# Two of three state corrections from TensorE matmuls to ScalarE products and VectorE sums, with a new instruction order

## Chip, cores, metric

The kernel runs on one core of a Trainium2 chip. The metric is the device time of one execution in microseconds (us). Shorter names, as the profile uses them: PE is TensorE (PEld its weight loads), DVE is VectorE, ACT is ScalarE, POOL is GpSimd, SP is SyncE, which issues nearly all DMAs.

## What is computed

Two independent layers over S = 2048 tokens of width D = 448, side by side in one output of width 896. All inputs and the output are bf16.

```
# A: sliding-window attention, 16 heads of 28; each token sees itself and 7 others, 2 tokens apart
qkv = x @ wqkv
logits = q . k[t - 2w] * 28**-0.5,  w = 0..7   (masked where t - 2w < 0)
a = (softmax(logits) . v[t - 2w]) @ wo
# B: a diagonal complex state-space layer with 448 states
dt = exp(log_dt); Lam_bar = exp(dt * Lam); B_bar = ((Lam_bar - 1) / Lam) * B
h[t] = Lam_bar * h[t-1] + B_bar @ x[t]
b = 2 * Re(C @ h[t]) + x * Dskip
out = concat(a, b)
```

## The kernel before, in words

Every piece of work is a small function marked `@op`, and the program is the list `ORDER`: a loop at the end of the kernel calls the functions in that order. In `QK021@32` the digits are arguments and what follows `@` are the PSUM banks; a trailing `.` lets ScalarE do an eviction, `=` lets VectorE do it. Each engine runs its own instructions strictly in the sequence in which `ORDER` emits them, and waits on semaphores for what other engines give. DMAs come from SP's queue in the same way. So the order of the list sets on every engine what is queued behind what, and a bank's next matmul waits for the eviction of the one before.

Layer A. `XI`, `XA`, `XH` transpose x on TensorE, `QK`, `QS` and `V_` project (line 244 and others), and `qk`, `qh`, `v` evict (all evictions carry line 114). `P` (line 379) multiplies q by shifted k on VectorE, 28 products of 128x2048 in a ring of seven buffers; `E_` (lines 391, 395) sums them over a head on TensorE. `lt` evicts the logits, `TD` transposes them by a DMA into `attn`, `sma`, `smb`, `smc` make the softmax (VectorE, ScalarE's Exp, VectorE). `AL` and `al` shift the weights into rows, `ad` writes them to DRAM, `sp` reads them back slanted as a band matrix into `PT`. POOL clears the targets first (`pm`, lines 873 to 877); `PT`, `oT`, `wo` and `ya` are in the pool `a_pt`, opened by `OP` in the space of the closed pools, which held `Cn` among others. `AV` (line 534) multiplies by v, `av` evicts, `W_` (line 547) is the output projection, `w` evicts, `ow` stores.

Layer B works on T = 4 tokens at a time: token 4i + j is step j of block i, and there are 512 blocks, 256 even and 256 odd. The 448 states are G = 7 groups of 64; a group has real and imaginary parts on 128 partitions.

- Setup: `PP`, `pa` to `pg` make small coefficients. For every group, `ty`, `tf` and `ts` make a table of cosines and sines: `ty` the phase of block n (ScalarE), `tf` the phase less its nearest whole number, in two VectorE instructions: a magic-number product `kM = n * f + 12582912`, whose rounding leaves a whole number (line 649), and a subtraction (line 650); `ts` takes Abs and Sin on ScalarE. `rb` k (line 666) makes `R[:, :, k]`, a 128x128 matrix per group that multiplies a state by Lam_bar to the power k + 1.
- `LC` loads C (lines 268, 269), `ci` copies it, `CD` transposes it by DMA into `Cw` (line 677), `ca` (ScalarE, line 684) and `cs` (VectorE, line 688) scale it. `BD` transposes B by DMA (line 672), `xt` transposes x of layer B into `xbuf` (line 696), `XR` loads that x again for the skip term, `xd` multiplies it by Dskip (line 797).
- `BU` makes B x of each step (line 244), `BR` (line 722) adds the rotated step before it, `z` evicts into `Z[:, g, j]` (steps 0 to 2) or `Z3` (step 3). `UP` and `y` fold an even block into its odd neighbour.
- `sa`, `sb`, `sd` are a scan over blocks on VectorE: turn into a rotating frame, a real scan (line 763), turn back. `DN` and `dn` (lines 775, 781) get the even blocks' end states.
- The correction: with the end state s of the block before, steps 0, 1 and 2 of every block need Lam_bar to the power j + 1 times s added. `H_` j g (line 788) is that rotation, one matmul of 128x512 with `R[:, g, j]`, and `h` j g (line 793) adds its PSUM result to `Z[:, g, j]` on VectorE: 21 of each.
- `C` j ct (line 807) multiplies 128 blocks of step j by `Cw`, seven matmuls summed over the groups; `c` (line 813) adds the skip term and `oc` stores. The last tile goes in two halves (`CH`, `ch`, `oh`, lines 827 to 842). A `C` of step j can run only when all seven `Z[:, g, j]` are corrected.

Of the kernel before, what the change touches and what calls it, by code (L numbers as in the profile page):

```python
# [25 lines left out]
OD, EV = 2, 2 + N2  # L26
SHR = 1.0 - 1e-6
MAGIC = 12582912.0
# [1 line left out]


ORDER = """
WU@0 XI0@0 xi00= xi01. XI1@1 XI2@2 xi10= xi11. PP@3 xi20. pcopy pa QS00@4 pb QS10@5 qk000. pd_ pc XH1@6 pe XA10@7
xh1. XA11@1 qk010. xa10= QK021@32 xa11. QK031@04 P000 ty0 QS01@6 pf QS11@5 P001 QK051@71 QK030 tf0 qk011. qk001. pg
ts00 QK050 qk031. ts10 ts20 QK020 qk051. P010 qk050. ty5 V_010@56 ty2 tf5 qk020. QK061@41 P011 V_001@73 ts05 V_011
V_000 v010. qk030. tf2 ts15 QK060 qk021= ts25 v000. P020 v001. QK040@50 qh001. rb2 v011. qh011. QK041 V_111@27 ty1
P021 V_101@36 V_110 qk040. qk041. tf1 ts02 E_00@50 P030 E_01 ts01 ts12 E_02 qh000. V_100 P031 qh010. v111. P040
QK130@41 ts22 ts11 v101. P041 v100. V_411@76 ts21 QK131 E_03 hc0 P050 ty6 E_04 ty4 V_410 qk131. tf6 qk130. QK100@31
P051 v411. ts06 v410. P060 QK110@46 ts16 BD v110. ts26 P061 QK101 ty3 QK151@72 QK111 qk100. E_05 rb0 qk101. E_06
qk110. QK150 tf4 lt00 P100 V_401@31 qk151. V_501@45 V_500 rb3 qk150. xt1 ts04 P101 lt01 QK120@27 ts14 qk111. tf3  # L40
v501. QK140@06 xt0 v500. P110 ts03 QK121 P111 QK141 qk120. QK161@54 V_400 qk140. xt3 P120 ts13 qk121. QK160 v400.
P121 qk141. v401. E_10@20 xt2 ts23 P130 E_11 ts24 V_510@73 qh101. P131 qh110. qh111. E_12 TD0 qh100. P140 E_13 hc1
V_511 P141 v511. v510. LC BU301@61 BU201@45 P150 BU300 sma0 BU200 OZ z30. XR BU400@37 z20. P151 smb0 BU000@64 P160
BR31 P161 BU001 ci1. BU401 E_14 z00. E_15 ci2= CD1 z40. E_16 rb1 z31. BR21 BR01 lt11 BU500@63 ci0= CD2 z21. smc0
z01. BU211@10 ci3. CD0 BU311@54 BU501 BU310 lt10 z50. CD3 BR32 BR41 BU210 z41. xd3 TD1 z32. BR51 xd2 BR22 AL0@2 z51.
BR33 z22. BU100@67 al0= z33. xd0 ca3 ad0 BU011@53 BU111@12 BU101 sma1 OP pm3 BU010 z10. pm0 wo UP3 AL1@6 cs3 smb1
BR11 xd1 BR02 BU110 z02. smc1 z11. BR03 al1. BR12 BU510@57 z03. ad1 z12. pm1 sp0 ca6 UP0 BR13 BU600@61 z13. y3. y0.
cs6 UP1 BR23 BU601 y1. z23. BU511 sa0 BU411@43 z60. BR52 pm4 ca1 BU410 sp1 sb0 BR61 z52. BR42 BU611@26 ca2 BU610 pm2
sd0 z61. AX@5 z42. BR53 BR62 AL2@1 ax= z53. z62. cs1 DN0@4 UP5 adx UP2 al2. DN1@5 BR43 dn0 BR63 y2. dn1 AL3@2 ad2
z63. sa2 H_10@1 y5. H_20@4 z43. H_11@0 al3. UP6 UP4 H_21@5 y6. H_00@7 ad3 y4. H_01@2 AV011@6 ca4 h21 spx AV010@3 h20  # L50
AV030@5 h01 av011. sp2 AV000@4 av010. cs2 AV020@6 av030. sb2 AV021@2 av000. AV001@3 av020. AV031@5 sd2 av001. W_00@4
sp3 av031. av021. W_20@6 ca5 h11 DN2@3 W_01@5 h00 DN3@2 dn2 w20. W_10@0 dn3 w01. sa4 ow20 W_11@7 ow01 W_21@3 w11.
w10. H_03@6 h10 H_02@2 w00. H_22@5 cs4 W_30@7 w21. ow00 sb4 H_23@0 ow21 H_13@1 w30. W_31@4 ow10 ca0 ow30 h13 AV100@3
ow11 h03 AV110@7 sd4 AV111@1 av110. AV131@6 av111. AV101@7 h02 av131. AV121@1 sa6 av101. AV130@6 av121. AV120@2 cs0
av130. DN5@7 av100. cs5 W_71@1 av120. dn5 W_61@6 w31. sb6 w71. h23 H_05@3 ow31 W_51@2 w61. ow71 ow61 W_41@7 w51= h05
H_15@4 ow51 H_25@1 W_50@0 h15 sd6 DN4@6 W_60@2 w50. w41. W_40@3 ow50 w60= ow41 DN6@4 C32@0 w40. ow60 dn6 dn4 ow40
h25 H_06@7 H_16@2 H_04@3 h06 H_12@4 H_14@6 h04 W_70@1 c32 H_24@7 C31@3 h22 oc32 w70= h12 C33@0 ow70 c31 h14 oc31
H_26@5 C30@1 c33 h26 oc33 h24 C02@4 c30 oc30 C20@3 c02 C00@6 c20 h16 oc20 CH0@0 c00 C01@5 oc00 C11@7 c01 ch0 oc01
C12@1 oh0 oc02 C13@4 C22@3 C03@2 c22 c12 oc22 c13 C21@6 oc12 c11 oc13 oc11 C10@5 c21 c03 oc21 CH1@0 oc03 c10 ch1
oc10 oh1  # L60
"""

@with_exitstack
def kernel(
# [17 lines left out]
    V = nc.vector  # L82
    ACT = nc.scalar
    PE = nc.tensor
    POOL = nc.gpsimd
    SP = nc.sync
# [4 lines left out]
    def pool(name, side="left", bufs=1, c=ctx):  # L91
        return c.enter_context(tc.tile_pool(name=name, bufs=bufs, side=side, reuse_waits="tile"))
# [3 lines left out]
    const = pool("const")  # L96
# [5 lines left out]
    keep = pool("b_keep", side="right")  # L102
# [80 lines left out]
    make_identity(nc, ident[:])  # L183
    iot = const.tile([128, N2], F32, tag="iota")
    POOL.iota(iot[:], [[1, N2]], base=0, channel_multiplier=0, allow_small_or_imprecise_dtypes=True)
    cols = const.tile([128, 5], F32, tag="cols")
    hpib, phi, sg, sscale = (cols[:, i:i + 1] for i in range(4))
    POOL.memset(hpib, 0.5 * PI * SHR)
    for col, lo, hi in ((phi, 0.0, 0.25), (sg, 2.0, -2.0), (sscale, 2 * PI * SHR, -2 * PI * SHR)):
        POOL.memset(col[0:64], lo)  # L190
        POOL.memset(col[64:128], hi)
# [34 lines left out]
    Ak0 = smp.tile([128, 2, 2560], BF16, tag="Ak0")  # L226
# [8 lines left out]
    pp = {}  # L235
# [162 lines left out]
    attn = smp.tile([128, NT, 128], BF16, tag="attn")  # L398
# [161 lines left out]
    def small(name, *shape):  # L560
        return const.tile([128, *shape], F32, tag=name, name=name)
    P3 = small("P3", 3, G)
    lre, lim, ld = (P3[:, i] for i in range(3))
    f1, rk, c1t, c2t, co, fT = (small(*a) for a in (("f1", G), ("rk", 5, G), ("c1t", G), ("c2t", G), ("co", T, 2, G), ("fT", G)))
# [78 lines left out]
        ACT.activation(pp["fr", g][:], iot[:], ACTF.Identity, scale=fT[:, g:g + 1])  # L643
# [147 lines left out]
    def h(j, g):  # L791
        zz = late["Z"][:, g, j, :]
        V.tensor_tensor(zz, pp.pop(("h", j, g))[:], zz, ALU.add)  # L793

    @op
    def xd(cb):
        V.tensor_tensor(xnB[:, cb], xnB[:, cb], dsk[:].unsqueeze(1).to_broadcast((128, T, D)), ALU.mult)  # L797
# [47 lines left out]
    late = {}  # L845
# [12 lines left out]
    @op  # L858
    def OP():
        cl.close()  # L860
        s6 = pool("a_pt")
        for n, shape in (("oT", (2, 4, 2, 512)), ("PT", (NS, H // HS, PW)), ("wo", (4, D)), ("ya", (6, D))):
            late[n] = s6.tile([128, *shape], BF16, tag=n, name=n)

        late["Ak"] = [late["oT"][:, 1].rearrange("p a b n -> p (a b n)")[:, 0:2560],
                      late["ya"].rearrange("p k n -> p (k n)")[:, 0:2560]]
        late["n"] = 0
# [17 lines left out]
    for step in ORDER.split():  # L885
        name, args, bank, e = re.fullmatch(r"([A-Za-z]+_?)(\d*)@?(\d*)([.=]?)", step).groups()
# [33 lines left out]
```

## Time and profile before

| | |
|---|---|
| runs | 132.95, 133.21, 133.34 us (median 133.21) |
| span of the profiled execution | 130.7 us; the profile gives no other time for this execution |
| what lies around the span, if it took what the runs took | 2.3 to 2.6 us |
| first and last TensorE matmul | 1.1 us, 127.8 us |
| ScalarE's last instruction ends | 104.8 us |
| VectorE's last instruction ends | 128.2 us |
| moved by DMA | 23.2 MB |

The span runs from the first to the last instruction of the program. A row of the profile names line, engine, operation, tiles and shapes, then the count, the busy time in all, the mean duration of one in ns, and the idle time of the engine before such instructions with what ended it. The matmuls' durations overlap; their pace is seen where a chain runs through many of them. In a table of stages each row is a stretch of the span: its length, then busy time and number of instructions of PE, PEld, DVE, ACT and POOL, then TensorE's granted clock (1.00 is full), the DMA share and GB/s.

### The profile page before, as it was taken

How to read it: one execution, taken by the hardware profiler on the slowest of the kernel's cores; microseconds unless marked ns; L12 is line 12 of the kernel's file. 1: busy time of each engine (PE TensorE's matmuls, PEld its weight loads, DVE VectorE, ACT ScalarE, POOL GpSimd, SP SyncE). 2: the span in 40 equal slices, each digit the busy share in tenths (PEclk: the TensorE clock that was granted, in tenths of full speed). 3: DMA queues.
4: the chain of work that ended last, by engine and by line, in shares of the span. 5: the costliest groups of instructions: out<-in, count | busy, mean ns of one | idle time of the engine just before them, and what ended most of it. 6: DMA issues, size and time to landing. Idle time of an engine off the chain costs nothing.

```text
span 130.7 us, 2869 instructions
## 1 busy us (share of the span) xinstructions
PE 125.4 (96%) x1067; PEld 62.2 (48%) x1067; DVE 113.4 (87%) x206; ACT 88.8 (68%) x185; POOL 19.8 (15%) x37
## 2 busy tenths in 40 slices
PE   6999999999999999999999999999899999999991
PEld 6543443434233334334454356854575555565550
DVE  5679999999999999999999899999997999752282
ACT  1779999999978996995979999997497300000000
POOL 6802000000000000200799920000000000000000
PEclk9999999999999999999999999999999999999999
DMA  3997989899999998999786999999412332213043
GB/s 116 238 207 174 326 230 167 197 197 258 139 259 210 212 200 187 310 303 209 209 200 222 185 169 293 255 179 185 141 54 70 105 105 94 87 55 103 0 146 118
DMA packets 47780, 23.24 MB, mean 178 GB/s; under 512 B 35639, under 2 KB 46711, under 8 KB 47767
## 3 DMA queue, kind: packets, MB, share of 16 engines
q1 hardware_dynamic: 47560, 23.03, 78.3%
q8 instruction: 8, 0.13, 0.4%
q10 hardware_dynamic: 207, 0.04, 0.2%
q14 instruction: 5, 0.04, 0.1%
HBM read 11.69 MB, written 6.37 MB: 138 GB/s over the span
## 4 chain that ended last, share of the span: by engine, by line
PE 80%; ACT 7%; DMA 6%; SPq 3%; issue 1%; DVE 0%; ACTq 0%
PE ps L244 38%; PE ps L807 15%; PE ps L547 6%; PE ps L534 5%; PE ps L391 5%; ACT ctmp L684 4%; DMA out_dram<-ya 3%; PE ps L722 3%; DMA wq<-in_A_wqkv_dram 3%; PE ps L788 3%; ACT Z L114 2%; SPq L128 2%; PE ps L348 1%; PE ps L827 1%; PE ps L395 1%
## 5 line engine op out<-in xcount | busy, mean ns | idle before, releaser
L379 DVE TENSOR_TENSOR pr<-qf,kf 128x2048 bf16<-128x2048 bf16 x24 | 28.7, 1236 | 0.1
L244 PE MATMUL ps<-xbuf,BT 128*128 128x512 bf16 (+1 forms) x112 | 23.6, 380 | 0.0
L244 PE MATMUL ps<-xT,wq 128*128 128x512 bf16 (+1 forms) x96 | 20.6, 380 | 0.1
L807 PE MATMUL ps<-Cw,Z 128*128 128x448 bf16 x105 | 20.5, 352 | 0.0
L114 ACT CAST Z<-ps 128x512 bf16<-128x512 f32 (+1 forms) x35 | 15.8, 520 | 3.0 <-PE ps L722 1.5
L813 DVE TENSOR_TENSOR xbuf<-ps,xnB 128x448 bf16<-128x448 f32 x15 | 9.0, 620 | 7.6 <-PE ps L807 7.5
L244 PEld LDWEIGHTS <-BT 128*128 128x128 bf16 (+1 forms) x112 | 8.9, 97 | 12.6 <-issue 3.5
L807 PEld LDWEIGHTS <-Z 128*128 128x128 bf16 x105 | 10.3, 98 | 9.4
L793 DVE TENSOR_TENSOR Z<-ps,Z 128x512 bf16<-128x512 f32 x21 | 13.7, 680 | 0.2 <-PE ps L788 0.2
L547 PE MATMUL ps<-wo,oT 128*128 128x448 bf16 x64 | 13.6, 353 | 0.0
L244 PEld LDWEIGHTS <-wq 128*128 128x128 bf16 (+1 forms) x96 | 7.8, 97 | 11.0 <-issue 2.3
L244 PE MATMUL ps<-wq,xT 128*128 128x448 bf16 (+1 forms) x64 | 13.0, 354 | 0.0
L877 POOL MEMSET PT<- 128x4320 f32 x3 | 11.0, 3698 | 7.2 <-DVE xnB L797 7.2
L114 ACT CAST ya<-ps 128x448 bf16<-128x448 f32 (+1 forms) x14 | 7.0, 566 | 5.5 <-PE ps L547 2.8
L684 ACT ACTIVATE ctmp<-Cw,c2t 64x448 f32<-64x448 bf16 x14 | 9.3, 667 | 0.3
L547 PEld LDWEIGHTS <-oT 128*128 128x128 bf16 x64 | 6.2, 98 | 5.7 <-ACT oT L114 0.2
L534 PE MATMUL ps<-PT,v_s 128*32 128x135 bf16 (+1 forms) x256 | 8.8, 298 | 0.0
L114 ACT CAST oT<-ps 128x512 bf16<-128x512 f32 x17 | 8.7, 620 | 0.1
L244 PEld LDWEIGHTS <-xT 128*128 128x128 bf16 (+1 forms) x64 | 4.8, 97 | 7.5 <-issue 4.1
L114 ACT CAST v_s<-ps 128x448 bf16<-128x448 f32 x16 | 8.2, 542 | 0.1
L534 PEld LDWEIGHTS <-v_s 128*32 128x32 bf16 x256 | 7.0, 110 | 0.7 <-ACT Z L114 0.4
L114 ACT CAST kf<-ps 128x512 bf16<-128x512 f32 x12 | 6.7, 582 | 0.7 <-PE ps L244 0.7
(150 smaller groups left out, 180.9 us busy)
## 6 DMA issues: line engine op xcount, KB each, us to landing
PT<-pd SPq DMA_DIRECT2D x16, 156.0 KB, 5.2
xnB<-in_B_x_dram SPq DMA_DIRECT2D x2, 896.0 KB
out_dram<-ya SPq DMA_DIRECT2D x16, 112.0 KB, 1.7
out_dram<-xbuf SPq DMA_DIRECT2D x15, 112.0 KB, 1.7
pd<-Ak SPq DMA_DIRECT2D x2, 640.0 KB, 3.5
xbuf<-in_A_x_dram SPq DMA_DIRECT2D x2, 448.0 KB
xnB<-in_B_x_dram SPq DMA_DIRECT2D x4, 224.0 KB, 5.4
xnB<-in_B_x_dram SPq DMA_DIRECT2D x4, 192.0 KB, 4.0
```

Source lines behind the costliest of these rows:

```text
L114: (ACT.copy if e == "A" else V.tensor_copy)(o, i)
L244: PE.matmul(o, l, r, start=(first and i == 0), stop=(not first and i == len(pairs) - 1 and not more[s]))
L379: V.tensor_tensor(t[:], q.unsqueeze(1).to_broadcast((128, 4, 512)), k4, ALU.mult)
L391: PE.matmul(acc[s][32 * i:32 * i + 32], E[:, f, ws, :], t[:, i, :], start=(f == 0 and ws == 0), stop=False)
L534: PE.matmul(p[32 * hh:32 * hh + 32, 128 * bl:128 * bl + n], v_s[:, t, 4 * hg + hh, :], PT[:, t % NS, (4 * hg + hh) // HS, (4 * hg + hh) % ...
L547: PE.matmul(p[:, 0:D], late["oT"][:, b // 4, hg, par, 128 * (b % 4):128 * (b % 4) + 128], late["wo"][:, hg, :], start=(hg == 0), stop=(hg ...
L684: ACT.activation(t[a:a + 64, 0:D], Cw[b:b + 64, g, :], ACTF.Copy, scale=c2t[a:a + 64, g:g + 1])
L722: PE.matmul(pp["z", g, j][:], rot(g, 0), late["Z"][:, g, j - 1, :], start=False, stop=True)
L793: V.tensor_tensor(zz, pp.pop(("h", j, g))[:], zz, ALU.add)
L807: PE.matmul(p[:, 0:D], z, Cw[:, g, :], start=(g == 0), stop=(g == G - 1))
L813: V.tensor_tensor(yo, pp.pop(("c", j, ct))[:, 0:D], xnB[:, ct, j, :], ALU.add)
L877: POOL.memset(late["PT"][:, 4 * i:4 * i + 4].rearrange("p t g n -> p (t g n)").bitcast(F32), 0.0)
```

## The change

Steps 1 and 2 of the correction no longer use TensorE. `sw` copies the end states with the two halves of the partitions swapped (real for imaginary) into `SW`, a part of `PT` that is free by then; eight DMAs on SP's queue. For each group and step, `hp` 0 is the state times the real part of the coefficient and `hp` 1 the swapped state times the imaginary part with its sign, both on ScalarE with a per-partition scale (`acol`, `bcol`, made once by `ab` on POOL), 28 products of 128x512. `hbuf` puts them into tiles that are free by then: `Ak0`, `attn`, and `PT` 8 to 11. `hy` g adds the two products of steps 1 and 2 in one VectorE instruction of 128x1024, `hz` g adds the sum to `Z[:, g, 1:3]`. `H_` and `h` are kept for step 0; `rb1` and `rb2` are no longer in the list.

The magic-number product becomes a function of its own, `tk`, which `ORDER` gives to ScalarE (g = 1, 4, 5, 6) or VectorE (0, 2, 3).

`ORDER` is new as a whole. Seven `z`, two `qh`, and one more each of `qk`, `v`, `av` and `al` go to VectorE; `ax`, one `ci` and one `xi` go to ScalarE. `LC` and three of the four `xt` come far earlier, ahead of `BD` and `TD0`. Six `ts` (`ts03`, `ts13`, `ts23`, `ts04`, `ts14`, `ts24`), of which four are Sin, now come after the Exp of `smb0`.

```diff
@@ -30,34 +30,34 @@
 
 
 ORDER = """
...
-V_511 P141 v511. v510. LC BU301@61 BU201@45 P150 BU300 sma0 BU200 OZ z30. XR BU400@37 z20. P151 smb0 BU000@64 P160
-BR31 P161 BU001 ci1. BU401 E_14 z00. E_15 ci2= CD1 z40. E_16 rb1 z31. BR21 BR01 lt11 BU500@63 ci0= CD2 z21. smc0
-z01. BU211@10 ci3. CD0 BU311@54 BU501 BU310 lt10 z50. CD3 BR32 BR41 BU210 z41. xd3 TD1 z32. BR51 xd2 BR22 AL0@2 z51.
-BR33 z22. BU100@67 al0= z33. xd0 ca3 ad0 BU011@53 BU111@12 BU101 sma1 OP pm3 BU010 z10. pm0 wo UP3 AL1@6 cs3 smb1
-BR11 xd1 BR02 BU110 z02. smc1 z11. BR03 al1. BR12 BU510@57 z03. ad1 z12. pm1 sp0 ca6 UP0 BR13 BU600@61 z13. y3. y0.
-cs6 UP1 BR23 BU601 y1. z23. BU511 sa0 BU411@43 z60. BR52 pm4 ca1 BU410 sp1 sb0 BR61 z52. BR42 BU611@26 ca2 BU610 pm2
-sd0 z61. AX@5 z42. BR53 BR62 AL2@1 ax= z53. z62. cs1 DN0@4 UP5 adx UP2 al2. DN1@5 BR43 dn0 BR63 y2. dn1 AL3@2 ad2
-z63. sa2 H_10@1 y5. H_20@4 z43. H_11@0 al3. UP6 UP4 H_21@5 y6. H_00@7 ad3 y4. H_01@2 AV011@6 ca4 h21 spx AV010@3 h20
-AV030@5 h01 av011. sp2 AV000@4 av010. cs2 AV020@6 av030. sb2 AV021@2 av000. AV001@3 av020. AV031@5 sd2 av001. W_00@4
-sp3 av031. av021. W_20@6 ca5 h11 DN2@3 W_01@5 h00 DN3@2 dn2 w20. W_10@0 dn3 w01. sa4 ow20 W_11@7 ow01 W_21@3 w11.
-w10. H_03@6 h10 H_02@2 w00. H_22@5 cs4 W_30@7 w21. ow00 sb4 H_23@0 ow21 H_13@1 w30. W_31@4 ow10 ca0 ow30 h13 AV100@3
-ow11 h03 AV110@7 sd4 AV111@1 av110. AV131@6 av111. AV101@7 h02 av131. AV121@1 sa6 av101. AV130@6 av121. AV120@2 cs0
-av130. DN5@7 av100. cs5 W_71@1 av120. dn5 W_61@6 w31. sb6 w71. h23 H_05@3 ow31 W_51@2 w61. ow71 ow61 W_41@7 w51= h05
-H_15@4 ow51 H_25@1 W_50@0 h15 sd6 DN4@6 W_60@2 w50. w41. W_40@3 ow50 w60= ow41 DN6@4 C32@0 w40. ow60 dn6 dn4 ow40
-h25 H_06@7 H_16@2 H_04@3 h06 H_12@4 H_14@6 h04 W_70@1 c32 H_24@7 C31@3 h22 oc32 w70= h12 C33@0 ow70 c31 h14 oc31
-H_26@5 C30@1 c33 h26 oc33 h24 C02@4 c30 oc30 C20@3 c02 C00@6 c20 h16 oc20 CH0@0 c00 C01@5 oc00 C11@7 c01 ch0 oc01
-C12@1 oh0 oc02 C13@4 C22@3 C03@2 c22 c12 oc22 c13 C21@6 oc12 c11 oc13 oc11 C10@5 c21 c03 oc21 CH1@0 oc03 c10 ch1
-oc10 oh1
+WU@0 XI0@1 xi00. xi01= XI1@2 XI2@3 xi10. xi11. PP@4 xi20. pcopy pa QS00@5 pb QS10@6 qk000. pd_ pc XH1@7 pe XA10@0 xh1.
+XA11@1 qk010= xa10= QK021@42 xa11. QK031@35 P000 ty0 QS01@6 pf QS11@7 P001 QK051@01 QK030 tk0= tf0 qk011. qk001= ty5
+QK020 tk5. QK050 LC xt2 xt3 xt0 qk030. QK041@76 P010 tf5 ts00 QK040 pg ab ts05 qk031. ts10 ts15 qk051. qk020. P011
+P020 ts20 qk021. tk2= V_101@35 V_100 ty2 tf2 qk041. ts25 ty1 tk1. ts02 qk050. V_001@14 P021 P030 ts12 tf1 V_000 v001.
+qk040. v100. BD E_00@23 P031 P040 QK060@60 V_010@47 V_011 QK061 v000. E_01 ts22 E_02 xt1 ty6 P041 E_03 P050 qh001.
+v011. qh000. rb0 qh011. hc0 v010. QK101@17 tk6. QK100 qk100. qh010. P051 QK110@64 QK161@10 QK111 P060 qk111. P061 ts01
+qk110. ts11 tf6 QK160 qh110= P100 v101. qk101. E_05 qh101. qh100= hc1 E_04 QK121@46 E_06 lt01 V_111@57 lt00 TD0 QK120
+qk120. qh111. qk121. QK131@32 P101 QK130 qk130. P110 P111 P120 QK140@14 QK151@06 qk131. ts21 P121 ci3. E_10@32 ts06
+ci1. CD1 P130 ci0. ci2= P131 ty4 V_110 QK150 qk150. QK141 qk140. CD0 P140 CD3 CD2 E_11 E_12 v111. V_511@01 v110. ts16
+qk141. V_510 tk4. qk151. P141 P150 P151 P160 v510. V_411@75 E_13 P161 V_410 v410. v411. ts26 ty3 V_500@46 V_501 v501.
+V_401@07 v511. v500. V_400 tf4 v401= rb3 E_14 E_15 E_16 lt11 BU401@56 lt10 TD1 BU201@14 sma0 smb0 BU400 BU100@72 BU200
+OZ OP pm0 pm2 z40= pm1 BR41 tk3= tf3 z20. smc0 v400. ca3 BU300@35 pm3 XR BU101 BU301 BU001@10 BR21 z21= z10. sma1
+BU000 z30. z00. BR31 z31. AL1@7 AL0@3 al0. ad0 al1. ad1 BR11 z11. BR01 z01= BU010@41 cs3 z41= smb1 smc1 BU110@53 ts03
+BU311@72 BU011 BU111 BU501@06 BR12 BR02 z12. BU500 z50= z02. ca6 xd3 BR03 z03. xd0 ts04 BR13 z13. ts13 sp0 pm4 BU310
+BR32 z32. AL2@5 UP0 BR51 z51. UP1 ts23 BU210@40 al2= cs6 y0. BR33 y1. AL3@7 sa0 BU511@65 BU211 ca1 BU411@13 cs1 al3=
+ts14 BR22 BU410 BR42 z42= sp1 z22. z33. ad2 wo BR23 BU510 UP3 BR43 AX@4 z23= ca2 ca4 UP2 BR52 AV010@7 ax. z52. y3.
+AV021@1 AV011@4 AV020@6 av021. z43. y2. av011. cs2 AV030@2 av020. ts24 av010. AV001@1 sb0 sd0 adx AV031@0 AV000@4 BR53
+UP4 av031. av000. av030. BU600@67 sa2 BU611@04 BU601 y4. z53. W_20@2 z60. sb2 sd2 DN1@3 av001. DN0@6 dn0 UP5 y5. sa4
+ad3 BR61 BU610 H_00@1 DN3@6 z61. BR62 DN2@5 dn2 ca5 spx W_01@7 sb4 dn3 cs4 W_11@5 z62. BR63 hp022 hp020 z63. W_21@0
+UP6 W_00@6 dn1 W_10@3 sd4 sp2 w20. w01. w11. H_03@2 hp012 w10. W_31@7 h00 h03 y6. w00. DN4@5 dn4 sa6 DN5@3 dn5 sb6 sd6
+ca0 w21. cs0 sp3 AV120@4 AV121@1 AV111@6 sw2 ow00 ow20 av111= sw4 sw0 av120. AV130@2 ow10 av121. av130. hp123 hp011
+AV131@5 AV100@0 AV110@3 av110. AV101@4 DN6@1 W_30@2 H_01@3 hp122 cs5 C32@6 hp024 h01 av131. dn6 xd2 w30= C30@3 av101.
+c30 C31@5 xd1 H_05@1 h05 W_61@4 c31 ow01 w31= hp013 av100. hp112 hp010 H_06@0 h06 W_50@2 ow21 hp120 hp015 H_02@3
+H_04@1 hp115 hp110 oc30 ow11 hy2 c32 W_71@5 W_41@7 ow31 hp113 hp114 hp111 hp021 hp125 C33@0 W_51@6 h02 hp014 w71=
+hp023 hp016 hp124 w61. h04 hp025 hy0 c33 hz2 sw6 hy3 C03@3 hp121 W_40@5 C01@1 hy4 w51. hz0 w50. oc32 C00@0 ow30 C02@4
+hz4 hy5 hz3 hz5 ow50 oc31 ow51 hy1 hz1 ow61 hp116 hp026 hp126 hy6 hz6 w41. c00 c01 ow71 ow41 W_60@6 W_70@2 w60. ow60
+w40. c02 w70. c03 oc01 oc33 oc00 oc02 ow40 oc03 C12@7 C11@6 C10@5 c10 c11 C13@0 c12 c13 oc12 C20@2 oc13 C21@1 c20 oc20
+c21 oc11 ow70 C22@4 c22 oc10 oc21 CH0@3 oc22 CH1@5 ch0 oh0 ch1 oh1
 """
 
 @with_exitstack
@@ -183,9 +183,10 @@
     make_identity(nc, ident[:])
     iot = const.tile([128, N2], F32, tag="iota")
     POOL.iota(iot[:], [[1, N2]], base=0, channel_multiplier=0, allow_small_or_imprecise_dtypes=True)
-    cols = const.tile([128, 5], F32, tag="cols")
+    cols = const.tile([128, 6], F32, tag="cols")
     hpib, phi, sg, sscale = (cols[:, i:i + 1] for i in range(4))
     POOL.memset(hpib, 0.5 * PI * SHR)
+    POOL.memset(cols[:, 5:6], MAGIC)
     for col, lo, hi in ((phi, 0.0, 0.25), (sg, 2.0, -2.0), (sscale, 2 * PI * SHR, -2 * PI * SHR)):
         POOL.memset(col[0:64], lo)
         POOL.memset(col[64:128], hi)
@@ -643,11 +644,17 @@
         ACT.activation(pp["fr", g][:], iot[:], ACTF.Identity, scale=fT[:, g:g + 1])
 
     @op
+    def tk(g, e):
+
+        kM = pp["kM", g] = keep.tile([128, N2], F32, tag="kM", name="kM")[:]
+        if e == "A":
+            ACT.activation(kM, iot[:], ACTF.Identity, bias=cols[:, 5:6], scale=fT[:, g:g + 1])
+        else:
+            V.tensor_scalar(kM, iot[:], fT[:, g:g + 1], MAGIC, ALU.mult, ALU.add)
+
+    @op
     def tf(g):
-
-        kM, fr = keep.tile([128, N2], F32, tag="kM", name="kM")[:], pp["fr", g][:]
-        V.tensor_scalar(kM, iot[:], fT[:, g:g + 1], MAGIC, ALU.mult, ALU.add)
-        V.scalar_tensor_tensor(fr, kM, MAGIC, fr, ALU.subtract, ALU.subtract)
+        V.scalar_tensor_tensor(pp["fr", g][:], pp["kM", g], MAGIC, pp["fr", g][:], ALU.subtract, ALU.subtract)
 
     @op
     def ts(i, g):
@@ -792,6 +799,57 @@
         zz = late["Z"][:, g, j, :]
         V.tensor_tensor(zz, pp.pop(("h", j, g))[:], zz, ALU.add)
 
+    acol, bcol = small("acol", T - 2, G), small("bcol", T - 2, G)
+
+    @op
+    def ab():
+
+        for o, k in ((acol, 1), (bcol, -1)):
+            for r, sl in enumerate((slice(0, 64), slice(64, 128))[::k]):
+                POOL.tensor_scalar(o[sl], co[sl, 1:T - 1, r], float(k), None, ALU.mult)
+
+    def seen(g, n=1, r=slice(0, 128)):
+
+        s = late["Z3"][r, g:g + n, OD - 1:OD - 1 + N2]
+        return bass.AP(s.tensor, s.offset, [list(s.ap[0]), *([list(s.ap[1])] if n > 1 else []), [EV - OD + 1, 2], [1, N2]])
+
+    @op
+    def sw(g0):
+
+        n = 2 if g0 < 6 else 1
+        for a, b in ((0, 64), (64, 0)):
+            o = late["SW"][a:a + 64, NC * g0:NC * (g0 + n)]
+            o = o.rearrange("p (g s n) -> p g s n", g=n, s=2) if n > 1 else o.rearrange("p (s n) -> p s n", s=2)
+            SP.dma_start(o, seen(g0, n, slice(b, b + 64)))
+
+    def hbuf(g, k):
+
+        if g < 2:
+            t, i = Ak0.rearrange("p k n -> p (k n)"), 2 * g
+        elif g == 2:
+            t, i = attn.rearrange("p t n -> p (t n)"), 0
+        else:
+            t, i = late["PT"][:, 8:12].rearrange("p t g n -> p (t g n)"), 2 * (g - 3)
+        return t[:, 2 * NC * (i + k):2 * NC * (i + k + 1)]
+
+    @op
+    def hp(k, j, g):
+
+        t = hbuf(g, k)[:, NC * (j - 1):NC * j]
+        if k:
+            ACT.activation(t, late["SW"][:, NC * g:NC * (g + 1)], ACTF.Copy, scale=bcol[:, j - 1, g:g + 1])
+        else:
+            ACT.activation(t.rearrange("p (s n) -> p s n", s=2), seen(g), ACTF.Copy, scale=acol[:, j - 1, g:g + 1])
+
+    @op
+    def hy(g):
+        V.tensor_tensor(hbuf(g, 0), hbuf(g, 0), hbuf(g, 1), ALU.add)
+
+    @op
+    def hz(g):
+        zz = late["Z"][:, g, 1:T - 1, :].rearrange("p j n -> p (j n)")
+        V.tensor_tensor(zz, zz, hbuf(g, 0), ALU.add)
+
     @op
     def xd(cb):
         V.tensor_tensor(xnB[:, cb], xnB[:, cb], dsk[:].unsqueeze(1).to_broadcast((128, T, D)), ALU.mult)
@@ -861,6 +919,7 @@
         s6 = pool("a_pt")
         for n, shape in (("oT", (2, 4, 2, 512)), ("PT", (NS, H // HS, PW)), ("wo", (4, D)), ("ya", (6, D))):
             late[n] = s6.tile([128, *shape], BF16, tag=n, name=n)
+        late["SW"] = late["PT"][:, 4:6].rearrange("p t g n -> p (t g n)")
 
         late["Ak"] = [late["oT"][:, 1].rearrange("p a b n -> p (a b n)")[:, 0:2560],
                       late["ya"].rearrange("p k n -> p (k n)")[:, 0:2560]]
```

More of the change, by code (lines that the diff above doesn't have):

```diff
@@ L32 @@
 ORDER = """
[L33 to L42, printed above, removed]
```

## The prediction

> **What bounds the kernel now.** I read the page first, then a table of stages, then the end of the chain of waits, then single rows.
>
> ```profile
> PE 125.4 (96%) x1067; PEld 62.2 (48%) x1067; DVE 113.4 (87%) x206; ACT 88.8 (68%) x185; POOL 19.8 (15%) x37
> ```
>
> TensorE (PE) is the first suspect, VectorE (DVE) the second. The table of busy time by stage (columns PE, PEld, DVE, ACT, POOL) shows where each is full:
>
> ```profile
> 0.00:10.00 10.00, 8.39 (x70) 5.55 (x71) 6.59 (x22) 5.40 (x15) 4.90 (x29) 1.00 0.74 184
> 10.00:60.00 50.00, 50.00 (x346) 19.39 (x345) 48.81 (x76) 46.31 (x97) 1.74 (x3) 1.00 1.05 225
> 60.00:100.00 40.00, 39.18 (x501) 22.48 (x500) 38.38 (x73) 35.21 (x71) 13.19 (x5) 1.00 0.86 182
> 100.00:113.00 13.00, 13.00 (x70) 6.65 (x68) 11.80 (x23) 1.87 (x4) 0.00 (x0) 1.00 0.33 107
> 113.00:130.70 17.70, 14.79 (x86) 8.10 (x83) 7.78 (x14) 0.00 (x0) 0.00 (x0) 1.00 0.27 84
> ```
>
> VectorE is as full as TensorE until 113 us: 105.6 busy, 7.4 idle, 3.4 of that in the first 10 us. It has room only in the last stage, where ScalarE has nothing to do. The clock column is 1.00 throughout. The chain's end (start, us, what) gives TensorE's pace:
>
> ```profile
> 116.52 10.59 PE ps L807 x56
> 127.12 0.68 PE ps L827 x7
> 127.80 0.02 issue
> 127.83 0.39 DVE xbuf L837
> ```
>
> One output matmul takes 10.59/56 = 0.189 us. From TensorE's end (127.8) to the span's end (130.7) it is 2.9 us. The runs of before took 132.95 to 133.34 us; the page gives no time of its own for the profiled execution, so I put 2.5 us around its 130.7 (to the median, 133.2). "Same" below means within 0.3%, 0.4 us, about what a measurement of this kernel can tell from no change.
>
> **The parts and their prices.** Durations are from these groups (busy, mean ns):
>
> ```profile
> L793 DVE TENSOR_TENSOR Z<-ps,Z 128x512 bf16<-128x512 f32 x21 | 13.7, 680 | 0.2 <-PE ps L788 0.2
> L666 DVE TENSOR_TENSOR R<-Is,co 128x896 bf16<-128x896 bf16 x4 | 4.3, 1080 | 0.0
> L425 DVE TENSOR_TENSOR attn<-attn,m 128x1024 bf16<-128x1024 bf16 x2 | 1.4, 692 | 0.1
> L684 ACT ACTIVATE ctmp<-Cw,c2t 64x448 f32<-64x448 bf16 x14 | 9.3, 667 | 0.3
> L643 ACT ACTIVATE fr<-iot,fT 128x256 f32<-128x256 f32 x7 | 3.4, 509 | 0.1
> ```
>
> A duration is not the pace: back to back, VectorE starts its next instruction 0.08 us before the last ends (in its timeline two L793 start at 111.01 and the next instruction at 112.21, so 0.60 each), ScalarE 0.1 us before. I use paces.
>
> TensorE: 14 of 21 H_ matmuls go (three in a row took 0.65 in the chain, 0.217 each): 14 x 0.217 = 3.0 us. With nothing else changed it ends at 127.8 - 3.0 = 124.8.
>
> VectorE, out: 14 h at 0.60 = 8.4; rb1 and rb2 (R of two steps is read by nothing now) 2.0; four magic products to ScalarE at 0.26 = 1.0; ax, a Cn copy and half an xT copy 1.2: 12.6 us. In: 7 hy and 7 hz, 1024 wide; L425 is that form, pace 0.61, so 8.5. The sums thus cost what the 14 corrections did; only the two rb are won. And the new order moves evictions from ScalarE to VectorE: nine of 512 columns (six z, one each of qk, av, al) at 0.60, two qh of 64 rows at 0.70, v401 0.54, z23 0.34: 7.7 us. Net 16.2 - 12.6 = +3.6: VectorE becomes fuller.
>
> ScalarE: 28 products of 128x512 with a scale column. L643 has such a scale and all 128 rows, 509 ns for 256 columns at pace 0.41; a plain eviction of 256 paces 0.265 and of 512 0.478, so 256 columns more are 0.21 and a product 0.62. L684 didn't overlap its neighbours (0.68 for 448 columns), which gives 0.73. I take 0.62, as L643 has the rows: 17.4 us (20.5 by the other). For that price alone the Trainium skill (ScalarE: Activation LUTs, What ACT_TABLE_LOAD costs) gives 186 ns + 0.833 per column + 93 for the scale column, less 93 of overlap: an estimate of 613 ns, 17.2 us in all. Four magic products add 1.6; the evictions handed over, less the three that come back, take off 5. Four Sin activations now stand behind smb0's Exp, so one more table load (L609's took 1283 ns): 1.3. Its work grows by 15, from 89 to 104 us; it had stood idle from 104.8 on, and the products lie between 85 and 113 us, where it has room. Their cover is thin only at the end: hp126 comes at about 110 to 113, and VectorE wants it at 115.
>
> POOL: ab is four instructions of 14 elements (a 64x1 memset took 92 ns, a 128x64 copy 238): under 1 us, needed 60 us later. SP: eight sw copies, 0.4 us of issue each, among output stores. LC and three of four xt are moved ahead of BD and TD0 (third rival).
>
> **The sum.** Which engine now sets the end? C12's last matmul needs hz6, and TensorE has little else left. VectorE's work up to hz6: 113.4 + 3.6 - 7.6 (eleven c at 0.62, two ch at 0.39) = 109.4 us busy. Idle until then: before's 7.4 less 1.9 spent waiting for TensorE or ScalarE (0.48, 0.81, 0.19 and 0.42, which a fuller VectorE won't have), plus 1.5 for new waits (smc0 now close behind smb0, al2 behind POOL's memsets): 7.0. hz6 ends at 116.4; with idle between 5 and 9, 114.4 to 118.4. Then TensorE has 43 matmuls at 0.189 and 14 half ones at 0.097: 9.5. It ends at 125.9. By its own queue it ends at 124.8 plus what it newly waits for VectorE (E_16 waits for the last P, about 1.8; AL for smc0, about 1.2) less old waits of about 2 that the same shift covers: 125.8. The two limits meet, so most of TensorE's 3.0 us isn't lost, but a third to a half is. Span 125.9 + 2.9 = 128.8, time **131.3 us**, 1.4% faster. Its own range is 130.6 to 132.3.
>
> **Rivals.**
>
> TensorE alone decides. VectorE's waits of 100 to 113 us vanish and nothing takes their place; the two-sided slack covers all. Then 124.8 + 2.9 + 2.5 = 130.2. For it: TensorE is full in the stages to 113 us. Against: VectorE's work before the last outputs grows by 3.6 us, and it had 1.2 us idle in 100 to 113.
>
> ScalarE's queue is blocked by a product. hp123 needs sw2, which needs dn2, dn3 and stands in SP's queue behind four sp3 copies; behind hp123 stand the evictions av110, av131, av101, and TensorE needs their banks. My reckoning: sw2 lands at 92, hp123's turn is at 94 to 95. The trace has such a case:
>
> ```profile
> ACT ya L114 <- DMA out_dram<-ya: 2.0, 1, 2.0
> ```
>
> One eviction waited 2.0 us for a store at 91 us, and TensorE lost 0.76 at 93. In the Trainium skill (TensorE: Matmul & The Clock Gate, the table at its head) ScalarE and VectorE run strictly first in, first out; that wait agrees. A wait of 1.5 us passed on to TensorE gives 132.8.
>
> The DMA order makes it slower. SP's timeline before:
>
> ```profile
> 31.11 5.15 SPq L672 DMA_TRANSPOSE BT<-Bn  x1
> 36.30 8.11 SPq L696 DMA_TRANSPOSE xbuf<-xnB  x4
> 44.46 1.86 SPq L413 DMA_TRANSPOSE attn<-lt  x1
> 54.69 6.40 SPq L677 DMA_TRANSPOSE Cw<-Cn  x4
> ```
>
> Now LC's loads (2.3 us of issue at 30.6) and the xt stand ahead, and the xt wait for the second half of B_x, which I put at 34 to 35. Then 8.1 + 5.2 + 1.9 + 6.4 bring the last Cw transpose to 56 to 57, landed at 58. POOL's memsets (PT began at 62.82, just after the Cw transposes) can start only there: 3 x 3.7 + 0.8 + 2.3 = 14.2, to 72. al2, now on VectorE, waits for the last of them, and VectorE reaches it at 71. If the transposes queue up behind LC's bytes (in before 6.6 us from issue to landing, at a DMA share of 1.05), the landing slips to 60 or 62 and VectorE stands for 3 to 5 us: 134.1 at 60.5. It decides from a landing after about 59.5, where the gain of 1.9 is gone. Against: the transposes as a whole start earlier than they did, because less stands idle between them.
>
> The change doesn't do what it says: the fuller pair of engines loses in many small waits what the matmuls save: 133.2.
>
> **Chances.** Forecast 0.42; TensorE alone 0.15; blocked products 0.18 (half of it within 0.3%); DMA order 0.20; nothing 0.05. Faster 0.42 + 0.15 + 0.09 = 0.66; same 0.13; slower 0.21. The range runs from TensorE alone to the DMA rival's middle: 130.0 to 134.0.
>
> **What would show it.** Right: TensorE's instruction count 14 lower; VectorE near 117 us busy and solid from 10 us to hz6 at 115.5 to 117.5; ScalarE near 104, products at 0.62 apart; TensorE ending near 126. TensorE alone: VectorE waiting for TensorE before hz6. Blocked products: ScalarE idle before L840 with evictions right behind. DMA order: VectorE idle before al2 near 71, POOL's last memset after 73. The forecast fails if a product paces much above 0.73, or if VectorE's idle to hz6 leaves 5 to 9 us.

## The result, and the profile after

The changed kernel took 131.53 us (median of 4 runs, 131.38 to 132.16), the kernel before 133.08 beside it: a ratio of 0.9896, 95% interval 0.986 to 0.9931. A second set on another chip gave 132.01 (131.61 to 132.49) against 133.12: 0.989 (0.9826 to 0.9954). The profiled execution took 131.58 us with a span of 129.9. The forecast was 131.3.

The first line of the changed kernel's page, and its table of stages (columns as before):

```profile
PE 122.3 (94%) x1044; PEld 60.6 (47%) x1053; DVE 116.4 (90%) x210; ACT 104.5 (80%) x208; POOL 20.9 (16%) x42
```

```profile
10.00:60.00 50.00, 48.94 (x332) 18.35 (x336) 48.60 (x73) 44.23 (x91) 4.22 (x7) 1.00 1.05 203
60.00:100.00 40.00, 38.67 (x502) 22.79 (x505) 37.77 (x78) 38.02 (x76) 11.71 (x6) 1.00 0.87 219
100.00:113.00 13.00, 13.00 (x70) 6.68 (x69) 12.89 (x22) 13.00 (x24) 0.00 (x0) 1.00 0.22 69
```

Weight loads fall from 1067 to 1053, which is the 14 matmuls less; the count of matmuls, 1044, is lower still because nine of their records are missing from the trace. Read the rows across, not the first line: the shares of the span still rank TensorE, VectorE, ScalarE, but from 100 to 113 us all three are full, ScalarE to the last hundredth. It had 1.87 us of work there before. The end of the chain of waits:

```profile
115.95 9.27 PE ps L865 x49
125.22 1.36 PE ps L885 x14
126.58 0.02 issue
126.60 0.39 DVE xbuf L895
```

TensorE ends at 126.58 instead of 127.80, and that is the gain: from there to the end of the execution it is 5.0 us after (131.58 - 126.58) and 5.1 before, taking for before the 2.2 us that its later runs have around their spans (the changed kernel's have 1.7; its span reaches further behind the last addition).

The new operations' rows (mean ns of one, idle time before them):

```profile
L840 ACT ACTIVATE PT<-PT,bcol 128x512 bf16<-128x512 bf16 x8 | 5.8, 746 | 0.0
L651 ACT ACTIVATE kM<-iot,cols,fT 128x256 f32<-128x256 f32 x4 | 2.4, 608 | 0.3
L846 DVE TENSOR_TENSOR PT<-PT 128x1024 bf16<-128x1024 bf16 x4 | 2.7, 684 | 0.1
L851 DVE TENSOR_TENSOR Z<-Z,PT 128x1024 bf16<-128x1024 bf16 x4 | 2.7, 687 | 0.0
```

In the timeline products follow each other every 0.613 us and sums every 0.60, as forecast (0.62 and 0.61). By the terms of the Trainium skill (ScalarE: Activation LUTs, What ACT_TABLE_LOAD costs) the prediction had an estimate of 613 ns for the product; the trace agrees.

Two waits that the prediction did not have, TensorE's and ScalarE's at 77 to 79 us:

```profile
PE ps L535 <- DMA PT<-pd: 0.9, 1, 0.9
```

```profile
ACT oT L114 <- PE ps L535: 1.0, 1, 1.0
```

TensorE comes to the attention product AV at 77 us and waits for the band's copies (they land at 77.8); ScalarE's next evictions are those of AV. The chain that ended last goes through this wait too: back from AV through the copies to POOL's clearing of `PT`. After it TensorE has only one more gap above 0.1 us (0.16 at 81.8). ScalarE pauses 0.19 us until 84.08, when a matmul gives it its next eviction, and is then solid until its products end at 114.7, but for one gap of 0.12 us at 85.2 and others of at most 0.03. At one place ScalarE's row touches VectorE's. ScalarE and then VectorE of the changed kernel around 110 us (start, duration):

```profile
109.61 0.73 ACT L840 ACTIVATE PT<-PT,bcol 128x512 bf16<-128x512 bf16 x1
110.22 0.54 ACT L114 CAST ya<-ps 128x448 bf16<-128x448 f32 x1
```

```profile
108.99 0.67 DVE L851 TENSOR_TENSOR Z<-Z,attn 128x1024 bf16<-128x1024 bf16 x1
109.59 1.47 DVE L846 TENSOR_TENSOR PT<-PT 128x1024 bf16<-128x1024 bf16 x2
110.98 0.68 DVE L851 TENSOR_TENSOR Z<-Z,Ak 128x1024 bf16<-128x1024 bf16 x1
```

The first line is hp124, the last product of group 4; it ends at 110.34. The two L846 together are hy3 and hy4 and take 1.47 us where two back to back take 1.29: hy4 started at 110.37, about 0.2 us later than its turn. From there VectorE is solid to hz6 at 116.73. C12's last matmul wants its result at 116.92: six matmuls of 0.189 after C12's first, which the timeline has at 115.79 (the chain counts from the end of the matmul before, 115.95).

### The profile page after: what moved, and what is told of

Same layout as the page of the kernel before. It is cut to its first block, busy times and chain, and to the rows that moved or that the text cites. A ratio compares the mean times of both kernels' runs of the same rounds, so it can differ in the third digit from the quotient of the medians.

```text
span 129.9 us, 2878 instructions
## 1 busy us (share of the span) xinstructions
PE 122.3 (94%) x1044; PEld 60.6 (47%) x1053; DVE 116.4 (90%) x210; ACT 104.5 (80%) x208; POOL 20.9 (16%) x42
## 4 chain that ended last, share of the span: by engine, by line
PE 58%; ACT 10%; DMA 8%; DVE 7%; POOLq 5%; SPq 4%; POOL 4%; issue 2%; ACTq 0%; DVEq 0%
PE ps L245 18%; PE ps L865 15%; PE ps L548 9%; PE ps L535 6%; POOLq L974 5%; DMA xbuf<-in_A_x_dram 4%; DMA PT<-pd 4%; POOL PT L936 4%; PE ps L392 3%; DVE pr L380 3%; SPq L504 3%; ACT v_s L114 2%; ACT kM L651 1%; PE ps L795 1%; PE ps L885 1%
## 5 line engine op out<-in xcount | busy, mean ns | idle before, releaser
L245 PE MATMUL ps<-xT,wq 128*128 128x512 bf16 (+1 forms) x93 | 21.2, 381 | 0.8 <-ACT kf L114 0.5
L114 ACT CAST Z<-ps 128x512 bf16<-128x512 f32 (+1 forms) x28 | 12.7, 494 | 0.4 <-PE ps L245 0.2
L245 PE MATMUL ps<-wq,xT 128*128 128x448 bf16 (+1 forms) x64 | 12.5, 355 | 0.0
L114 ACT CAST v_s<-ps 128x448 bf16<-128x448 f32 x15 | 7.5, 538 | 0.8 <-PE ps L245 0.8
L114 ACT CAST ya<-ps 128x448 bf16<-128x448 f32 x13 | 6.6, 542 | 1.0 <-DMA out_dram<-ya 0.8
L114 ACT CAST qf<-ps 128x512 bf16<-128x512 f32 x11 | 6.5, 590 | 0.5 <-PE ps L350 0.4
```

Of the source, the lines that this page charges most:

```text
L114: (ACT.copy if e == "A" else V.tensor_copy)(o, i)
L245: PE.matmul(o, l, r, start=(first and i == 0), stop=(not first and i == len(pairs) - 1 and not more[s]))
```

## The experiments

### Is it VectorE, TensorE, or both?

VectorE relieved, TensorE relieved, and both (`...` stands for steps left out here):

```diff
-dn6 xd2 w30= ... C31@5 xd1 H_05@1
+dn6 w30= ... C31@5 H_05@1
```

```diff
-        for g in range(G):
+        for g in range(3 if j == 3 else 0, G):
```

> The changed kernel without two of its four skip products (two VectorE products of 128x1792, 1.0 us each at pace, at 99.7 and 101.7 us; their rows of x go unscaled into the output). VectorE has 2.0 us less to do ahead of its last state correction, which ends at 116.73 in the changed kernel. Theory 'two limits that meet' (TensorE reaches the first output group that needs the last correction at 115.95 and its matmul that needs it at 117.1): TensorE's own queue now holds the end, time falls by 0 to 0.4, 131.1 to 131.5. Rival 'VectorE alone sets the end': falls by 2.0, 129.5. Rival 'TensorE's queue alone': as the theory here, 131.4.

> The changed kernel with the four output groups of step 3 summed over four of seven state groups (12 matmuls of 0.189 us left out, 2.27 us, all ahead of the outputs that need the last correction; the outputs of step 3 lack three groups). Theory 'two limits that meet': TensorE comes to 113.7 and waits for the last correction at 116.73, after which 42 full and 14 half matmuls follow (9.3 us), end 126.2 instead of 126.58: time falls by 0.4, to 131.1. Rival 'TensorE's queue alone': falls by 2.3, to 129.3. Rival 'VectorE alone': no change, 131.5.

> Both omissions together (two skip products and 12 output matmuls). Theory 'two limits that meet': the last correction ends at 114.7, TensorE waits for it from 113.7 and ends at 124.2; time falls by 2.2 to 2.4, to 129.2, though neither omission alone brought more than 0.4. Rival 'TensorE's queue alone': 129.3, as with its matmuls alone left out. Rival 'VectorE alone': 129.5, as with its products alone left out.

Measured against 132.94 for the kernel before: 131.94 (0.9908, 0.9873 to 0.9942), 131.92 (0.9904, 0.9852 to 0.9956), 132.05 (0.9925, 0.9896 to 0.9953). The first two are no faster than the changed kernel's two sets, 131.53 and 132.01, as the theory had it (by the figures they lie 0.4 and 0.8 above its range); that TensorE alone or VectorE alone decides is refuted. But the third refutes the theory too: 2 us off both engines brought nothing. The timelines of that run, ScalarE and then VectorE, name the third party:

```profile
109.05 0.74 ACT L842 ACTIVATE PT<-Z,acol 128x512 bf16<-128x512 bf16 x1
109.66 0.74 ACT L840 ACTIVATE PT<-PT,bcol 128x512 bf16<-128x512 bf16 x1
```

```profile
107.88 0.68 DVE L851 TENSOR_TENSOR Z<-Z,attn 128x1024 bf16<-128x1024 bf16 x1
109.20 0.69 DVE L846 TENSOR_TENSOR PT<-PT 128x1024 bf16<-128x1024 bf16 x1 [0.64 <-ACT PT L842]
110.43 0.69 DVE L846 TENSOR_TENSOR PT<-PT 128x1024 bf16<-128x1024 bf16 x1 [0.53 <-ACT PT L840]
```

VectorE reaches hy3 and hy4 early and waits 0.64 and 0.53 us for ScalarE's products; hy4 starts within 0.06 us of the changed kernel's. TensorE, early too, waits 0.87 us at 114.3 for the bank of the eviction w41, which stands behind the last product, and then 0.21 us for hz6. In this profile and in that of TensorE relieved it waits once more behind hz6, 0.36 and 0.51 us at about 119, for an eviction that a late store held up (last section); without that, by an estimate from these waits, the two would have been about half a us shorter, still far from 129.2.

### Three limits?

> The changed kernel without the four ScalarE products of group 5 (4 x 0.61 us at pace; that group's correction is wrong). The two omissions run before, alone and together, moved the time by less than 0.5, and where both were made TensorE waited 0.9 us at 114.3 for a ScalarE eviction that stands behind the last product. New theory 'three limits that meet': the first late output group (C12) needs a bank that ScalarE's eviction w41 frees at 115.1, TensorE reaches it at 115.8, and VectorE's last correction is wanted at 116.9 and ends at 116.7. So this omission alone moves nothing: 131.0 to 131.6. Rival 'ScalarE's queue alone sets the end': falls by 2.4, to 129.1.

> All three omissions together (two skip products on VectorE, 12 output matmuls on TensorE, four products on ScalarE), and three steps moved: the eviction w41 one product earlier, the stores of two finished rows ahead of the store that waits for ScalarE. Theory 'three limits that meet': each engine comes to the late outputs 2.0 to 2.4 us earlier, time 129.2 to 129.5, though no omission alone and no pair brought it. Rival 'something else that none of these touches' (a transfer, the start): 131.0 or more.

The first takes `hp015 hp025 hp115 hp125` out of the order. The second has all three omissions and these moves:

```diff
-ow50 oc31 ow51 hy1 hz1 ow61 hp116 hp026 hp126 hy6 hz6 w41. c00 c01 ow71 ow41
+ow71 ow61 ow50 oc31 ow51 hy1 hz1 hp116 hp026 w41. hp126 hy6 hz6 c00 c01 ow41
```

Measured against 133.10: ScalarE alone relieved 132.58 (0.9954, 0.9927 to 0.9982), no faster, and 1 us above what was expected (in its profile TensorE had waited 1.4 us for a transpose of x at 53 us, which the omission can't have caused). All three 130.13 (0.98, 0.9775 to 0.9826), 1.4 us below the changed kernel's 131.53 and 1.9 below its second set. Beside it the same three moves without any omission took 132.35 (under Small moves), so the three omissions brought 2.2 us and the moves alone nothing. The two omissions of TensorE and VectorE together with the moves were not run; that these still need ScalarE's share rests on the times below. The expectation of 129.2 to 129.5 was 0.6 to 0.9 too good: VectorE was relieved least and comes last again, though by 0.2 us only. The end of this run's chain:

```profile
114.25 1.14 PE ps L865 x6
115.39 0.02 issue
115.41 8.31 PE ps L865 x43
```

Six matmuls of C12, a short wait, and the seventh right behind hz6, which ended at 115.35.

Times of one link in each trace settle it (us from the span's start; the pause is the one that ends at 84.08 in the changed kernel):

| kernel | pause ends | hp124 ends | hy4 starts | hz6 ends |
|---|---|---|---|---|
| changed | 84.08 | 110.34 | 110.37 | 116.73 |
| changed, second set | 84.67 | 110.93 | 110.97 | 117.33 |
| VectorE relieved | 83.51 | 109.78 | 109.81 | 116.16 |
| TensorE relieved | 84.32 | 110.58 | 110.61 | 116.97 |
| both relieved | 84.13 | 110.39 | 110.43 | 116.78 |
| ScalarE relieved | 85.32 | 109.74 | 111.42 | 117.78 |
| all three relieved | 84.21 | 108.63 | 108.99 | 115.35 |

In the first five ScalarE takes 26.26 or 26.27 us from the pause to hp124, hy4 follows within 0.04 and hz6 6.35 or 6.36 after hy4's start, whatever VectorE or TensorE had been spared. Only in the last two, with ScalarE relieved, does hy4 follow hy3 in VectorE's own row instead (hy3 ended at 111.51 and 109.08, 0.09 after hy4's start, as back to back). With ScalarE alone relieved hz6 comes 32.46 us after the pause, against 32.65 in the changed kernel. So ScalarE's products set the last correction, VectorE by itself would be ready about 0.2 us earlier, and TensorE wants the result 0.2 us later. The start of the interval isn't ScalarE's own: a matmul ends the pause, 83.51 to 85.32 us in these traces.

### Is ScalarE really full?

```diff
-z40= z21= z01= z41= z50= z42= z23= al2= qk001= av111= qh110= qh100= v401=
+z40. z21. z01. z41. z50. z42. z23. al2. qk001. av111. qh110. qh100. v401.
```

> The changed kernel with 13 of the evictions that its order hands to VectorE given back to ScalarE (seven z, al2, qk001, av111, two of qh, v401): VectorE -7.1 us at pace, ScalarE +6.2. Theory 'ScalarE is one of three limits': it is full from 96 to 114.7 and at 38.0 of 40 us in 60 to 100, so evictions come late, TensorE waits for banks and the last product ends 2 to 4 us later: 133 to 135. Rival 'VectorE alone sets the end, ScalarE has room': the last sum 5 us earlier, TensorE's queue holds: 131.2.

135.96 against 133.12 (1.0158, 1.0076 to 1.024): 4 us slower than the changed kernel's second set, and 1 us beyond the theory's range; the rival's 131.2 is refuted. VectorE's longest waits from 50 to 100 us in the profile of this run (an execution of 137.17 us; the other three took 134.91 to 136.00):

```profile
DVE z L436 <- ACT attn L430: 4.6, 2, 4.0
DVE Cw L695 <- ACT ctmp L691: 2.7, 1, 2.7
```

VectorE had 7.5 us less to do (108.9 busy for 116.4) and stood for the second Exp of the softmax, which ScalarE reached at 66.7 us instead of 62.7; TensorE waited 2.5 us for ScalarE's evictions of `Z`, as expected. So ScalarE has no room for these evictions. Most of the loss shown here lies from 55 to 80 us, ahead of the products: what the room among the products alone is worth this run doesn't show.

### The products without the order, and the order without the products

> The kernel before with the new corrections in its old order of steps: 14 matmuls, 14 additions and two rotation tables out; 28 ScalarE products, 14 wide VectorE sums and the swap copies in, each put behind what it needs; all evictions, magic products and DMAs as before. By the prediction's terms TensorE's own end is 124.8, VectorE has 2.0 less to do and keeps its evictions. Theory 'the order is part of the price': in the old order groups 4 to 6 are ready last (dn4 at about 104, swap copy 2.3 us later), ten products of 0.61 follow, so the last sum ends at 114 to 118 and the time is 131.5 to 134. Rival 'the products alone bring it, the order adds nothing': 130.2 to 131.0.

> The changed kernel's order with the old corrections: 14 matmuls and 14 VectorE additions in place of the products and the two wide sums of each group, the rotation tables of both steps again, no swap copies. TensorE +3.0 us, VectorE +2.0 - 0.1, ScalarE -17.4. By the prediction's terms: TensorE's end 126.58 + 3.0 = 129.6, VectorE's last correction 118.7; time 134.0 to 134.6, slower than the kernel before (133.1), since the new order hands evictions to VectorE that only the products on ScalarE call for. Rival 'the order is worth something by itself': 133.1 or less.

144.58 (1.0727, 1.0623 to 1.0831) and 139.0 (1.0455, 1.0427 to 1.0484), both far beyond what either theory gave. In the first, `rb1 rb2` and every `H_` and `h` of steps 1 and 2 go, `sw` follows the `dn` of its groups, `hp` stands among ScalarE's evictions, and `hy hz` where the later inputs are ready; the second is the reverse:

```diff
-hy0 ... hz0
+H_10@3 ... h10 ... H_20@4 ... h20
```

Where each step stands was chosen by hand. In the old order products stand ahead of evictions in ScalarE's queue, and TensorE waits for these. Its longest waits there, from 84 us on, and a row of the table of stages:

```profile
PE ps L865 <- DVE xbuf L871: 2.6, 1, 2.6
PE ps L529 <- ACT oT L114: 2.3, 3, 1.5
PE ps L782 <- ACT ya L114: 2.3, 1, 2.3
```

```profile
100.00:113.00 13.00, 9.52 (x93) 5.02 (x93) 9.01 (x17) 10.74 (x22) 0.00 (x0) 0.77 0.17 55
```

This is near the prediction's rival of the blocked products, but not the same: the evictions wait for products that run, not for one that stands (the longest wait of a product for a swap copy is 0.66 us, at 117). The Trainium skill (TensorE: Matmul & The Clock Gate, the table at its head) has ScalarE and VectorE as strictly first in, first out; the trace agrees, with waits of up to 2.3 us. The longest wait of all, 2.6 us at 120.5, is for VectorE, whose output additions stand behind sums that need the last products. A part of the time is TensorE's clock: it was granted at 0.83 from 100 to 130 us of this profile (an execution of 145.87 us), with TensorE busy for 23.5 of the 30 us, so by an estimate 4 us (23.5 x 0.17) are the clock's; over the four runs its mean was 0.964 to 0.988, against 0.996 to 1.000 in the changed kernel.

With the old corrections in the new order matmuls and additions get in each other's way (the profile is of an execution of 142.65 us, the other three took 138.91 to 139.05): around 119 to 122 us three additions wait 0.85 us each for a matmul that stands behind seven output matmuls, and from 123 to 125.5 TensorE waits 0.2 to 0.6 us at a time for additions that free its banks. Neither figure prices the change: they show that each half loses in these two orders, not what the best order for either half would give.

### Small moves

> The changed kernel with three steps moved and nothing left out: the eviction w41 ahead of the last product instead of behind it, and the stores ow71 and ow61, whose rows are ready at 104.4 and 110.8, ahead of ow50, for which SP's queue stood idle from 107.3 to 112.9. Theory: ScalarE's side of the three limits loosens by 0.6 (w41) and its 0.84 us wait for a store buffer goes, but TensorE's own queue and VectorE hold the end: 131.2 to 131.6, with fewer late runs. Rival 'ScalarE's queue alone': 130.7.

> The changed kernel once more, beside the runs of this call, since the kernel with three moved steps came out at 132.35 on another chip and its profile had lost time in places that the moves do not touch (0.7 us on TensorE at 96 us, a store issue of 1.9 us at 98). If these belong to the kernel and not to the moves, this run shows some of them again, with 131.4 to 132.4; if the moves caused them, 131.4 to 131.6.

> The changed kernel with one DMA moved: the transpose of B (BD) ahead of the three transposes of x that wait for a load (SP's queue stood idle from 29.4 to 33.4 us before them). All later transposes come about 2 us earlier, so ScalarE's 2.5 us wait for the first probability transpose at 50.4 goes and POOL's clearing begins at 55.7 instead of 57.7. Theory 'three limits at the late outputs': these waits are covered, time within 0.3 of the changed kernel. Rival 'the transposes' order holds the chain' (the prediction's DMA rival turned round): 0.9 to 1.5 faster, 130.0 to 130.6.

The first makes the three moves shown above and nothing else, the second changes nothing, and the third is

```diff
-LC xt2 xt3 xt0 ... v100. BD E_00@23
+LC BD xt2 xt3 xt0 ... v100. E_00@23
```

The three moved steps: 132.35 (0.996, 0.9941 to 0.9979). The kernel as it is: 132.01, and in its profile a swap copy's issue of 1.2 us at 97. B's transpose moved ahead: 132.02 (0.9884, 0.9835 to 0.9932). So sets of the changed kernel lie 0.5 us apart by themselves, and moves of this size can't be told from none. In the last the premise failed: BD began at 33.1, not 31.1, took 6.0 us instead of 4.8, and the last C transpose was issued at 55.61 instead of 55.64.

> The reference's computation with all three limits loosened by order alone: the moves of the run beside it; a second buffer for lt (ScalarE waited 2.5 us for the first one's transpose) with the evictions z40 and z21 and the magic product of group 3 given back to ScalarE (VectorE -1.5 us); the second load of B_x issued behind the two stores of the probability band instead of ahead of them, and POOL clearing the band's second third before its third, so that the band's copies land before TensorE comes to them (it waited 0.9 us). Theory 'three limits that meet': TensorE's 0.9 us decide, 130.5 to 130.9. Rival 'TensorE's waits move elsewhere': 131.5.

It makes the same three moves, and besides:

```diff
-name="lt", bufs=1)
+name="lt", bufs=2)
-pm0 pm2 z40= pm1 BR41 tk3= ... XR ... z21= ... ad1
+pm0 pm1 pm2 z40. BR41 tk3. ... z21. ... ad1 XR
```

142.38 us (140.43 to 143.19), a plain miss. VectorE's and TensorE's longest waits in this run:

```profile
DVE xnB L855 <- DMA xnB<-in_B_x_dram: 8.5, 1, 8.5
```

```profile
PE ps L245 <- DVE oT L114: 7.3, 1, 7.3
```

Issued at 65 to 66.8 us behind the band's stores, the second load of B_x (1.8 MB) shared the queue with the band's copies and landed at 77.8; VectorE stood for it with al2 behind it in its queue, and the first band copies, 77.8 in the changed kernel, landed at 83.4. After its 7.3 us of waiting TensorE's granted clock was 0.50 from 80 to 84 us, where it was busy for 3.35, so by an estimate another 1.7 us are the clock's; in the changed kernel's profile it is 1.00 in every stage. What the 77.8 us landing of the copies costs in the changed kernel is therefore still not measured; a move that makes it earlier without this wasn't tried. One trace gives a hint. With VectorE relieved the order is the same up to 99 us, yet in that execution the copies held TensorE for 0.21 us and not 0.92, and the pause, hz6 and TensorE's end (126.02 us) came 0.56 to 0.57 us earlier.

## Why the prediction was right, point by point

**TensorE.** 14 matmuls of 0.217 went, and 1.2 of the 3.0 us arrived at its end; the forecast was 1.9. By the stages it is idle 0.2 us more in the first 10, 1.06 more from 10 to 60 and 0.5 more from 60 to 100. That new waits would take a part held, but 60% and not "a third to a half", and not where it was put: neither E_16 nor AL waited 0.2 us. What came, from 10 us on, is 0.92 for the band's copies at 77.9, 0.55 for an eviction of kf at 22.6 and four of 0.14 to 0.16; the old waits that went were 0.85, not 2.

**VectorE.** Busy 116.4 for a forecast 117, idle 7.3 up to hz6 for 7.0, hz6 at 116.73 for 116.4. The parts held: corrections, sums, evictions, magic products.

**ScalarE: the step that failed.** Its work was right (104.5 for 104; one table load more, 1.28 us at 63.8), and so was the product. Wrong was that the products lie "between 85 and 113 us, where it has room". ScalarE in that stretch of the kernel before, and all engines after:

```profile
85.00:113.00 28.00, 14.23 (x28) 1.00 0.51 114
```

```profile
85.00:113.00 28.00, 28.00 (x287) 16.11 (x285) 27.29 (x55) 27.74 (x52) 0.00 (x0) 1.00 0.50 109
```

Before, 13.8 of the 28 us were idle, and 28 products at 0.62 are 17.4. The new order took some of the other work away, but the products still did not fit: the last ended at 114.69 instead of 110 to 113. VectorE's hy4 waited about 0.2 us for one of them, and with both other engines relieved it came no earlier. The prediction looked at the last product's cover (hp126, 0.6 us early for hy6) and not at hp124, which had none.

**The sum.** TensorE ended 0.7 us later than forecast, and what follows it took 5.0 instead of 5.4: 131.58 for 131.3. "The two limits meet" was the right form, with a third that the prediction held to be covered. That the number is so close is in part luck: hz6 comes out alike by VectorE's row and by ScalarE's, which the prediction didn't reckon with, and the two errors at the end have opposite signs. Its chances don't quite add up as listed: half of the blocked products and "nothing" make 0.14 for the same time, not 0.13, and 0.20 for slower.

**Rivals.** TensorE alone: refuted, by the run with its matmuls relieved. Blocked products: not here, hp123 began at 96.05 with no gap before it; in the old order evictions waited behind products, though not behind one that stood for long. DMA order: it didn't make the kernel slower, for the last C transpose was issued by 55.6 and POOL cleared from 57.7 to 71.7, ahead of the deciding 59.5 and 73; al2 waited 0.24 us. But POOL's clearing and the band's copies behind it do lie on the chain that ended last, with 0.92 us of TensorE's time.

## What to carry to other kernels

Work moved to an engine "with room" must be summed against that engine's idle time in the stretch between its inputs and its reader, not against its share of the span; one row of busy time for that stretch of the kernel before has the answer. When two engines are relieved together and nothing moves, look for a third queue that is solid from one event to the next: an interval that is the same to 0.01 us in several traces points to it, and relieving that queue too is the test. And for each consumer check the cover of every product it reads, since an early one in a solid queue can be later than its reader while the last still looks safe.

## What was not expected of the hardware

SP's issues of output stores and swap copies, mostly 0.3 to 0.7 us each, took 1.1 to 1.9 us at 94 to 100 us in nine of the twelve later profiles and 1.8 to 2.3 at 112 to 116 in three of them, with nothing waited for that the trace shows; in the changed kernel's first profile the longest was 0.9. In the run with TensorE relieved, one at 114.0 (2.28 us) made the next stores land late, ScalarE's eviction w40 waited 2.9 us for its buffer and TensorE 0.5 for the bank; with both relieved, one at 114.3 (1.83 us) did the same, with 2.7 and 0.36. Five profiles also show TensorE standing 0.19 to 0.74 us at 96.3 to 96.8 us among the short AV matmuls with no releaser. The cause of either stays open; they are of the size by which sets of this kernel differ.
